# First expert layer of a mixture-of-experts kernel in seven block products, with seeded PSUM banks and streamed block sums

## The chip, the cores and the metric

The kernel runs on one core of a Trainium2 chip. The metric is the device time of one execution in microseconds (us); I quote medians. TensorE is called PE below, VectorE DVE, ScalarE ACT, GpSimd POOL, the sequencer that issues transfers SP, as in the profile.

## The reference

Linear attention produces x of 4608 x 512, an eight-round normalisation gives each token a weight P for each of 8 experts, and every token goes through every expert:

```python
out = np.zeros((N, D), dtype=np.float32)          # N = 4608, D = 512
for e in range(E):                                # E = 8
    h = np.maximum(x @ w1[e], 0.0)                # w1[e]: 512 x 1024   "first layer"
    ye = h @ w2[e]                                # w2[e]: 1024 x 512   "second layer"
    out += P[:, e:e + 1] * ye
```

The two products per expert are nearly all of the work. The kernel computes in fp16 with fp32 sums.

## The kernel before

The work of the experts is cut into units: one expert, one group of 512 tokens, so 72 units. In experts 1 to 7 the second layer is already done as a two-by-two block product with seven block products in place of eight (Strassen's scheme in Winograd's form): sums of blocks of h and w2 are formed first (`S` and `T`), and one accumulated PSUM bank may serve several output blocks. (PSUM holds the sums that PE makes; a bank is one 128 x 512 fp32 tile of it here. To evict a bank is to read its result out.) The first layer is plain, with x held transposed on chip (`xT`):

```python
def layer1(e, g):
    ...
    for f in range(NFT):                           # 8 feature tiles of 128
        def f_hq(_, ...):
            for c in range(NDT):                   # 4 contraction tiles of 128
                nc.tensor.matmul(ghq["tile"], lhsT=gw1["tile"][:, c, ts(f, P)],
                                 rhs=xT[c][:, ds(512 * g, 512)], start=(c == 0), stop=(c == NDT - 1))
        def f_rl(_, ...):
            nc.scalar.activation(out=gh["tile"][:, f, :], in_=ghq["tile"], func=AF.Relu)
        t1 = add(("pe", 0.87), f_hq, deps=[...], acq=[ghq], use=[gw1], prio=...)
        ...
```

The second layer runs twice per unit, once for each half of the tokens (`sub(0)`, `sub(1)`), each half in two banks of its own. VectorE evicts with one instruction that scales by P and adds into the accumulator in SBUF:

```python
def sub(s):
    gX, gY = S_.grp(p_ye[2 * s]), S_.grp(p_ye[2 * s + 1])
    ...
    m1 = pm(A(1, 1), Bq(1, 1), X, True, th[0:4], True, 0.0);   e1 = ev(X, 0, 0, m1)
    m5 = pm(SS(1), T(1), Y, True, [tS[0]], True, 0.1);         e5 = ev(Y, 1, 1, m5)
    m2 = pm(A(1, 2), Bq(2, 1), Z, False, ...);                 ev(Z, 0, 0, m2)
    m6 = pm(SS(2), T(2), X, False, [tS[1], e1], ...);          e6 = ev(X, 0, 1, m6)
    ...                                            # m3, m7, m4: 7 products, 7 evictions per half
```

Nobody writes the order of instructions down. Each `add` records a task with an engine, an assumed duration and its dependencies, and a planner in the kernel plays the tasks through and emits them in the order in which they would start. The semaphores are put in afterwards, from what each emitted instruction reads and writes; for PSUM they go by whole banks.

The softmax here doesn't subtract the row's maximum and nothing guards it: scores larger than these inputs give would overflow.

Of the kernel before, what the change touches and what calls it, by code (L numbers as in the profile page):

```python
# [8 lines left out]

# [107 lines left out]
def kernel(  # L117
# [36 lines left out]
    sk = ctx.enter_context(tc.tile_pool(name="sk", bufs=1))  # L154

    xT = [const.tile([P, N], FP16, tag=f"xT{c}", name=f"xT{c}") for c in range(NDT)]
# [18 lines left out]
    p_T, p_S = S_.pool(2), S_.pool(2)  # L175
# [48 lines left out]
    def att(b, g):  # L224
# [140 lines left out]
        for c2 in range(2):  # L365
            gx = S_.grp(p_att)

            def f_xt(_, c2=c2, gx=gx):
                gx["tile"] = aps.tile([P, S], FP16, tag="att", name="xt_ps")
                for i in range(5):  # L370
                    nc.tensor.transpose(gx["tile"][:, 64 * js[i]:64 * js[i] + P],  # L371
                                        gxn["tile"][:, i, 2 * c2:2 * c2 + 2, :].rearrange("p r e -> p (r e)"), ident)

            def f_xc(e, c2=c2, gx=gx):
                copy(e, xT[2 * g + c2][:, S * b:S * b + S], gx["tile"])
            t1 = fadd(("pe", 0.3), f_xt, deps=txn, acq=[gx], use=[gxn], prio=pr)
            xt_done[(b, 2 * g + c2)] = fadd({"act": 0.64, "dve": 0.46}, f_xc, deps=[t1], use=[gx], prio=pr)

    lg_done = []

    def logits(b2):
        gl = S_.grp(p_att)

        def f_l(_):
            gl["tile"] = aps.tile([P, NJ, E], FP32, tag="att", name="lg_ps")
            for i in range(NJ):
                for c in range(NDT):
                    nc.tensor.matmul(gl["tile"][:, i, :], lhsT=xT[c][:, ts(NJ * b2 + i, P)], rhs=wg_sb[:, c, :],  # L388
                                     start=(c == 0), stop=(c == NDT - 1))

        def f_x(_):
            nc.scalar.activation(out=P0_sb[:, NJ * b2:NJ * b2 + NJ, :], in_=gl["tile"], func=AF.Exp)
        t1 = add(("pe", 1.0), f_l, deps=[xt_done[(b, c)] for b in (2 * b2, 2 * b2 + 1) for c in range(NDT)],
                 acq=[gl], prio=-50.0)
        lg_done.append(add(("act", 0.3), f_x, deps=[t1], use=[gl], prio=-50.0))
# [85 lines left out]
    accp = []  # L481

    def f_close(_):
        front.close()
        accp.append(ctx.enter_context(tc.tile_pool(name="accp", bufs=1)))
        for g in range(NA, NG):
            acc[g] = accp[0].tile([P, 4, 512], FP32, tag=f"acc{g}", name=f"acc{g}")
        accp.append(ctx.enter_context(tc.tile_pool(name="combo", bufs=2)))
    t_close = add(("none", 0.0), f_close, deps=front_ids, prio=0.0)
# [6 lines left out]
    def layer1(e, g):  # L496
        gw1, tw1, gw2, tw2 = w_t[e]
        ui = e * NG + g
        bs = range(512 * g // S, (512 * g + 511) // S + 1)
        xd = [xt_done[(b, c)] for b in bs for c in range(NDT)] if e == 0 else []  # L500
        th = []
        gh = S_.grp(p_h)

        def f_ha(_):
            gh["tile"] = hpool.tile([P, NFT, 512], FP16, tag="h", name="h")
        tha = add(("none", 0.0), f_ha, deps=[prev_hq[0]], acq=[gh], prio=ui - 400.0)
        for f in range(NFT):
            use_att = e > 0 and f % 2 == 1
            ghq = S_.grp(p_att if use_att else p_hq)

            def f_hq(_, f=f, ghq=ghq, use_att=use_att):
                ghq["tile"] = (aps if use_att else hqp).tile([P, 512], FP32, tag="att" if use_att else "hq", name="hq")
                for c in range(NDT):
                    nc.tensor.matmul(ghq["tile"], lhsT=gw1["tile"][:, c, ts(f, P)], rhs=xT[c][:, ds(512 * g, 512)],  # L514
                                     start=(c == 0), stop=(c == NDT - 1))

            def f_rl(_, f=f, ghq=ghq):
                nc.scalar.activation(out=gh["tile"][:, f, :], in_=ghq["tile"], func=AF.Relu)  # L518
            t1 = add(("pe", 0.87), f_hq, deps=[tw1[f // 4], prev_hq[0]] + xd, acq=[ghq], use=[gw1], prio=ui + 0.1 * f + 0.35)
            prev_hq[0] = t1  # L520
            th.append(add(("act", 0.6), f_rl, deps=[t1, tha], use=[ghq, gh], prio=ui - 400.0))
        return gh, th
# [10 lines left out]
    def unit_plain(e, g):  # L533
        gw1, tw1, gw2, tw2 = w_t[e]
        gh, th = layer1(e, g)
        gy = [S_.grp(p_ye[tt % 2]) for tt in range(4)]
        ty = [None] * 4
        for tt in range(4):
            for half in range(2):
                def f_y(_, half=half, tt=tt):  # L540
                    if half == 0:
                        gy[tt]["tile"] = yps.tile([P, 512], FP32, tag=f"ye{tt % 2}", name=f"ye{tt % 2}")
                    for f in range(4 * half, 4 * half + 4):
                        nc.tensor.matmul(gy[tt]["tile"], lhsT=gh["tile"][:, f, ds(P * tt, P)], rhs=gw2["tile"][:, f, :],  # L544
                                         start=(f == 0), stop=(f == NFT - 1))
                ty[tt] = add(("pe", 0.87), f_y, deps=[tw2[half], ty[tt]] + th[4 * half:4 * half + 4],
                             acq=[gy[tt]] if half == 0 else [], use=[gw2, gh],
                             prio=e * NG + g + 0.1 * (2 * tt + half) + 0.65)
# [25 lines left out]
    def combos(e):  # L574
        gw1, tw1, gw2, tw2 = w_t[e]
        gT = S_.grp(p_T)
        last = None
        for i in range(4):
            def f_T(_, i=i):
                if i == 0:  # L580
                    gT["tile"] = accp[1].tile([P, 4, 4, 256], FP16, tag="T", name="T")
# [6 lines left out]
            last = add(("dve", 0.6), f_T, deps=tw2 + [t_close, last], acq=[gT] if i == 0 else [], use=[gw2, gT],  # L588
                       prio=NG * e - 4.0)
        return gT, last  # L590

    def unit(e, g, gT, tT):
        gw1, tw1, gw2, tw2 = w_t[e]
        ui = e * NG + g
        gh, th = layer1(e, g)
        gS = S_.grp(p_S)
        tS = []
        for i in range(4):
            def f_S(_, i=i):
                if i == 0:  # L600
                    gS["tile"] = accp[1].tile([P, 4, 4, 2, P], FP16, tag="S", name="S")
# [7 lines left out]
            tS.append(add(("dve", 0.62), f_S, deps=th + tS[-1:] + [t_close], acq=[gS] if i == 0 else [],  # L609
                          use=[gh, gS], prio=ui - 399.0))  # L610
        def sub(s):
            gX, gY = S_.grp(p_ye[2 * s]), S_.grp(p_ye[2 * s + 1])
# [13 lines left out]
            def pm(lhs, rhs, region, first, deps, acq, prio):  # L626
                g_, col = region

                def f_m(_):
                    if acq:  # L630
                        n = 2 * s + (0 if g_ is gX else 1)
                        g_["tile"] = yps.tile([P, 2, 256], FP32, tag=f"ye{n}", name=f"ye{n}")
                    for kk in range(4):
                        nc.tensor.matmul(g_["tile"][:, col, :], lhsT=lhs(kk), rhs=rhs(kk),  # L634
                                         start=(first and kk == 0), stop=(kk == 3), skip_group_check=True)
                return add(("pe", 0.44), f_m, deps=tw2 + [tT] + deps, acq=[g_] if acq else [],
                           use=[gw2, gT, gh, gS, g_], prio=ui + 0.3 + prio + 0.02 * s)

            def ev(region, ti, dh, dep):
                g_, col = region  # L640
                gg = 4 * g + 2 * s + ti

                def f_e(_):
                    dst = acc[g][:, 2 * s + ti, 256 * dh:256 * dh + 256]
                    nc.vector.scalar_tensor_tensor(out=dst, in0=g_["tile"][:, col, :], scalar=P_sb[:, gg, e:e + 1],  # L645
                                                   in1=dst, op0=ALU.mult, op1=ALU.add)
# [3 lines left out]
            X, Z, Y = (gX, 0), (gX, 1), (gY, 0)  # L650
            m1 = pm(A(1, 1), Bq(1, 1), X, True, th[0:4], True, 0.0)
            e1 = ev(X, 0, 0, m1)
            m5 = pm(SS(1), T(1), Y, True, [tS[0]], True, 0.1)
            e5 = ev(Y, 1, 1, m5)
            m2 = pm(A(1, 2), Bq(2, 1), Z, False, th[4:8] + [m1], False, 0.05)
            ev(Z, 0, 0, m2)
            m6 = pm(SS(2), T(2), X, False, [tS[1], e1], False, 0.2)
            e6 = ev(X, 0, 1, m6)
            m3 = pm(SS(4), Bq(2, 2), Y, False, [tS[3], e5], False, 0.3)
            ev(Y, 0, 1, m3)  # L660
            m7 = pm(SS(3), T(3), X, False, [tS[2], e6], False, 0.4)
            e7 = ev(X, 1, 1, m7)
            m4 = pm(A(2, 2), T(4), X, False, th[4:8] + [e7], False, 0.6)
            ev(X, 1, 0, m4)
# [6 lines left out]
    w_t[1] = load_w1(1, prio=0.0, after=60.0) + load_w2(1, prio=0.0, after=70.0)  # L671
    for e in range(E):
        if e >= 2:
            w_t[e] = load_w1(e, prio=float(e), deps=w_t[e - 1][1][1:]) + load_w2(e, prio=float(e), deps=w_t[e - 1][3][1:])
        if e > 0:
            gT, tT = combos(e)
        for g in range(NG):
            if e == 0 or (e == E - 1 and g == NG - 1):
                unit_plain(e, g)
            else:  # L680
                unit(e, g, gT, tT)
# [31 lines left out]
```

## Time and profile before

| | before |
|---|---|
| time, median (lowest to highest) | 1029.81 us (1029.41 to 1031.32, 4 runs) |
| PE busy, share of the profiled span | 98% |
| DVE, ACT, POOL busy | 69%, 42%, 4% |
| a steady unit | 13.02 us |

A busy PE in this profile includes a tail of about 0.17 us after each group of matmuls (1.04 us are shown for eight that are followed by the next after 0.87). The pace must be read from starts, and the time from one start to the next that leaves no gap is called a slot below. Between the products whose bank is evicted and reused, the kernel before has first-layer matmuls to put. This is its timeline right after the product called N6 below (columns: start, duration, engine, line, operation, operands, count):

```profile
506.31 1.03 PE L514 MATMUL hq<-xT,w 128*128 128x512 f16 x4
507.17 1.04 PE L634 MATMUL ye<-w,S 128*128 128x256 f16 x8
508.04 1.04 PE L634 MATMUL ye<-T,S 128*128 128x256 f16 x8
```

N6 ended its slot at 506.31; N7, the third line, starts 1.73 us later. The first two lines are independent work that fills the eviction's time.

### The profile page before, as it was taken

How to read it: one execution, taken by the hardware profiler on the slowest of the kernel's cores; microseconds unless marked ns; L12 is line 12 of the kernel's file. 1: busy time of each engine (PE TensorE's matmuls, PEld its weight loads, DVE VectorE, ACT ScalarE, POOL GpSimd, SP SyncE). 2: the span in 40 equal slices, each digit the busy share in tenths (PEclk: the TensorE clock that was granted, in tenths of full speed). 3: DMA queues.
4: the chain of work that ended last, by engine and by line, in shares of the span. 5: the costliest groups of instructions: out<-in, count | busy, mean ns of one | idle time of the engine just before them, and what ended most of it. 6: DMA issues, size and time to landing. Idle time of an engine off the chain costs nothing.

```text
span 1033.2 us, 17328 instructions
## 1 busy us (share of the span) xinstructions
PE 1014.5 (98%) x7202; PEld 646.7 (63%) x7202; DVE 713.9 (69%) x1501; ACT 432.4 (42%) x714; POOL 41.6 (4%) x47
## 2 busy tenths in 40 slices
PE   7898999999999999999999999999999999999998
PEld 3554664466666666666666666666666666666664
DVE  6897958566666766676666766676666766666664
ACT  4886844543333333333333333333333333333332
POOL 4221100000000000000000000000000000000000
PEclk9898999999999999999999999999999999999999
DMA  9997400140005000040005000050004100013333
GB/s 263 341 257 255 150 2 1 17 66 2 1 1 83 1 1 2 4 79 1 1 1 79 3 1 1 1 83 1 1 1 64 19 1 1 1 31 81 80 81 98
DMA packets 31743, 55.65 MB, mean 54 GB/s; under 512 B 2736, under 2 KB 11952, under 8 KB 31664
## 3 DMA queue, kind: packets, MB, share of 16 engines
q0 software_dynamic: 14480, 20.33, 11.4%
q1 hardware_dynamic: 16864, 33.69, 10.7%
q8 instruction: 56, 0.92, 0.4%
q10 hardware_dynamic: 320, 0.52, 0.1%
q14 instruction: 23, 0.19, 0.1%
HBM read 61.88 MB, written 9.44 MB: 69 GB/s over the span
## 4 chain that ended last, share of the span: by engine, by line
PE 92%; DVE 4%; DMA 2%; ACT 1%; issue 0%; DVEq 0%; ACTq 0%
PE hq L514 47%; PE ye L634 37%; PE ye L544 5%; DMA kin<-in_k_dram 2%; PE qt_ps L316 1%; PE num_ps L355 1%; PE xt_ps L371 1%; PE kv_ps L290 1%; DVE xn L360 1%; DVE tq L266 1%; DVE gs L420 0%; PE lg_ps L388 0%; PE den_ps L331 0%; PE cs_ps L425 0%; DVE eq L264 0%
## 5 line engine op out<-in xcount | busy, mean ns | idle before, releaser
L518 ACT ACTIVATE h<-hq 128x512 f16<-128x512 f32 x576 | 343.5, 597 | 548.5 <-PE hq L514 548.3
L514 PE MATMUL hq<-xT,w 128*128 128x512 f16 x2304 | 560.9, 381 | 0.2 <-ACT h L518 0.2
L645 DVE SCALAR_TENSOR_TENSOR acc<-ye,P_sb,acc 128x256 f32<-128x256 f32 x868 | 391.3, 484 | 143.3 <-PE ye L634 143.3
L514 PEld LDWEIGHTS <-w 128*128 128x128 f16 x2304 | 225.0, 98 | 199.8 <-issue 5.4
L634 PEld LDWEIGHTS <-S 128*128 128x128 f16 x1984 | 194.1, 98 | 48.9
L634 PE MATMUL ye<-T,S 128*128 128x256 f16 x1488 | 192.8, 273 | 0.0
L634 PEld LDWEIGHTS <-h 128*128 128x128 f16 x1488 | 145.6, 98 | 57.6
L608 DVE TENSOR_TENSOR S<-h 128x1024 f16<-128x1024 f16 x124 | 85.5, 689 | 112.3 <-ACT h L518 112.3
L634 PE MATMUL ye<-w,h 128*128 128x256 f16 x992 | 129.4, 273 | 0.0
L544 PE MATMUL ye<-w,h 128*128 128x512 f16 x320 | 79.2, 385 | 0.0
L634 PE MATMUL ye<-T,h 128*128 128x256 f16 x496 | 65.1, 273 | 0.0
L634 PE MATMUL ye<-w,S 128*128 128x256 f16 x496 | 64.3, 273 | 0.0
L544 PEld LDWEIGHTS <-h 128*128 128x128 f16 x320 | 30.3, 99 | 32.3 <-issue 1.4
L608 DVE TENSOR_TENSOR S<-h,S 128x1024 f16<-128x1024 f16 x62 | 42.5, 686 | 0.0
L608 DVE TENSOR_TENSOR S<-S,h 128x1024 f16<-128x1024 f16 x62 | 42.3, 682 | 0.0
L194 POOL DMA_DIRECT2D w<-in_moe_w_dram x18 | 14.9, 829 | 665.7 <-PE hq L514 628.5
L360 DVE TENSOR_TENSOR xn<-num_ps,rden 128x512 f16<-128x512 f32 (+1 forms) x48 | 26.7, 596 | 5.3 <-PE num_ps L355 4.8
L212 POOL CAST vv<-vin 128x1152 f16<-128x1152 f32 x16 | 21.2, 1325 | 85.8 <-DMA vin<-in_v_dram 63.0
L561 DVE TENSOR_SCALAR acc<-acc,P_sb 128x512 f32<-128x512 f32 x36 | 15.1, 490 | 12.4 <-ACT acc L208 12.3
L253 ACT ACTIVATE ek<-kin 128x1152 f16<-128x1152 f32 x16 | 18.6, 1161 | 8.7 <-DMA kin<-in_k_dram 8.6
L208 ACT COPY acc<-ye 128x512 f32<-128x512 f32 x27 | 15.8, 586 | 14.7 <-PE ye L544 14.7
L355 PE MATMUL num_ps<-kvz,qpT 128*128 128x128 f16 x160 | 15.9, 230 | 4.8 <-DVE rden L337 3.7
(66 smaller groups left out, 327.1 us busy)
## 6 DMA issues: line engine op xcount, KB each, us to landing
w<-in_moe_w_dram POOLq DMA_DIRECT2D x14, 1024.0 KB, 9.5
out_dram<-acc SPq DMA_DIRECT2D x68, 128.0 KB, 2.3
kin<-in_k_dram SPq DMA_DIRECT2D x14, 576.0 KB, 6.9
qin<-in_q_dram SPq DMA_DIRECT2D x14, 576.0 KB, 5.8
vin<-in_v_dram SPq DMA_DIRECT2D x14, 576.0 KB, 6.8
w<-in_moe_w_dram POOLq DMA_DIRECT2D x4, 512.0 KB, 7.8
kin<-in_k_dram POOLq DMA_DIRECT2D x2, 576.0 KB, 11.5
qin<-in_q_dram POOLq DMA_DIRECT2D x2, 576.0 KB, 12.2
```

Of the source, the lines that this page charges most:

```text
L208: nc.scalar.copy(out=dst, in_=src)
L212: nc.gpsimd.tensor_copy(out=dst, in_=src)
L253: nc.scalar.activation(out=ge["tile"], in_=gin[nm]["tile"], func=AF.Exp)
L355: nc.tensor.matmul(gn["tile"][:, i - i0, :, hh, :], lhsT=gq["tile"][:, hh, js[i]:js[i] + 2, :].rearrange("p j w -> p (j w)"), rhs=gz["tile ...
L360: nc.vector.tensor_tensor(out=gxn["tile"][:, i0:i1], in0=gn["tile"][:, 0:i1 - i0].rearrange("p i r h e -> p i (r h) e"), in1=grd["tile"][: ...
L514: nc.tensor.matmul(ghq["tile"], lhsT=gw1["tile"][:, c, ts(f, P)], rhs=xT[c][:, ds(512 * g, 512)], start=(c == 0), stop=(c == NDT - 1))
L518: nc.scalar.activation(out=gh["tile"][:, f, :], in_=ghq["tile"], func=AF.Relu)
L544: nc.tensor.matmul(gy[tt]["tile"], lhsT=gh["tile"][:, f, ds(P * tt, P)], rhs=gw2["tile"][:, f, :], start=(f == 0), stop=(f == NFT - 1))
L561: nc.vector.tensor_scalar(out=acc[g][:, tt, :], in0=acc[g][:, tt, :], scalar1=P_sb[:, gg, 0:1], scalar2=None, op0=ALU.mult)
L608: nc.vector.tensor_tensor(out=Sx[:, i], in0=a0, in1=a1, op=op)
L634: nc.tensor.matmul(g_["tile"][:, col, :], lhsT=lhs(kk), rhs=rhs(kk), start=(first and kk == 0), stop=(kk == 3), skip_group_check=True)
L645: nc.vector.scalar_tensor_tensor(out=dst, in0=g_["tile"][:, col, :], scalar=P_sb[:, gg, e:e + 1], in1=dst, op0=ALU.mult, op1=ALU.add)
```

## The change

The intent: one eighth of the first layer's matmul work goes in 63 of 72 units. The parts:

- First layer in seven products of blocks of 256 tokens (`block7`), in two pairs of feature tiles. Sums of w1 blocks (`W`) are made on VectorE once per expert, sums of x blocks once in expert 0, written to a DRAM scratch (`xd`) and loaded again for every unit, in place of keeping x on chip.
- A product that serves two output blocks (M1, N1) is no longer read twice: ScalarE copies its bank into a second PSUM bank ("seed"), and the next product accumulates on the copy.
- Both token halves of the second layer now share banks (`ye0`, `ye1`, and one seeded bank), because the first layer needs a seeded bank too and the kernel, as before, has eight banks in use.
- Three of fourteen evictions a unit go over ScalarE (scaled copy to SBUF) and GpSimd (add).

The core of the diff, cut:

```diff
-    xT = [const.tile([P, N], FP16, ...) for c in range(NDT)]
+    xT = xp.tile([P, NDT, N], FP16, tag="xT", name="xT")
+    xd = [dpool.tile([P, NXB], FP16, tag=f"xd{g}", name=f"xd{g}") for g in range(NG)]     # in DRAM
...
+    def x_load(e, g):
+            nc.sync.dma_start(out=gr["tile"], in_=xd[g])                    # 128 x 3584 fp16
...
+    def block7(e, g, gW, tW):
+        def pair(gi):
+            m1 = pm(A(1, 1, gi), B11, gX, True, ...)
+            a1 = acts(f_seed, [m1], [gX], [gZ])            # nc.scalar.copy(out=Zt[1], in_=gX["tile"])
+            m5 = pm(W(1, gi), T(1), gR, True, [m1, tW], 0.05)
+            a5 = acts(f_s5, [m5, ...], [gR], [gs5])        # copy to SBUF
+            m2 = pm(A(1, 2, gi), B21, gZ, False, [a1], 0.1)
+            th[0].append(acts(f_h11, [m2], [gZ, gh]))      # relu
+            m6 = pm(W(2, gi), T(2), gX, False, [a1, tW], 0.08)
+            a2 = acts(f_s2, [m6, ...], [gX], [gs2])        # copy to SBUF
+            m3 = pm(W(4, gi), B22, gR, False, [a5], 0.12)
+            th[1].append(add(("dve", 0.8), f_h12, deps=[m3, a2], ...))      # add and relu
+            m7 = pm(W(3, gi), T(3), gX, False, [a2], 0.14)
+            d22 = add(("dve", 0.8), f_h22, deps=[m7, a5], ...)              # add and relu
+            m4 = pm(A(2, 2, gi), T(4), gX, False, [d22], 0.16)
+            th[0].append(acts(f_h21, [m4], [gX, gh]))      # relu
+        pair(0)
+        pair(1)
...
-            e1 = ev(X, 0, 0, m1)
+            c1 = add(("act", 0.48), f_seed, deps=[m1], acq=[gZ], use=[gX], prio=ui - 400.0)
-            ev(Z, 0, 0, m2)
+            ev(gZ, 0, 0, m2, split=True)                   # over ScalarE and GpSimd
...
-            ev(X, 1, 0, m4)
+            ev(gX, 1, 0, m4, split=(s == 1))
```

## The prediction

> **What bounds the kernel now.** I read the busy table first, then the chain that ended last, then a stretch of the timeline in the middle of the run. The page of the kernel before says:
>
> ```profile
> PE 1014.5 (98%) x7202; PEld 646.7 (63%) x7202; DVE 713.9 (69%) x1501; ACT 432.4 (42%) x714; POOL 41.6 (4%) x47
> ...
> PE hq L514 47%; PE ye L634 37%; PE ye L544 5%; DMA kin<-in_k_dram 2%; PE qt_ps L316 1%; PE num_ps L355 1%; PE xt_ps L371 1%; PE kv_ps L290 1%; DVE xn L360 1%; DVE tq L266 1%; DVE gs L420 0%; PE lg_ps L388 0%; PE den_ps L331 0%; PE cs_ps L425 0%; DVE eq L264 0%
> ...
> L514 PE MATMUL hq<-xT,w 128*128 128x512 f16 x2304 | 560.9, 381 | 0.2 <-ACT h L518 0.2
> L645 DVE SCALAR_TENSOR_TENSOR acc<-ye,P_sb,acc 128x256 f32<-128x256 f32 x868 | 391.3, 484 | 143.3 <-PE ye L634 143.3
> ```
>
> TensorE (PE) carries the chain and hardly waits: 0.2 us in front of 2304 first-layer matmuls (L514). A full PE can still be a stalling one, so the timeline of a steady unit (one expert, 512 tokens) has to show the pace. The columns are start, duration, engine, line, operation, count:
>
> ```profile
> 501.96 1.04 PE L634 MATMUL ye<-w,h 128*128 128x256 f16 x8
> 502.21 0.60 ACT L518 ACTIVATE h<-hq 128x512 f16<-128x512 f32 x1 [0.32 <-PE hq L514]
> 502.60 1.79 DVE L645 SCALAR_TENSOR_TENSOR acc<-ye,P_sb,acc 128x256 f32<-128x256 f32 x4
> ...
> 502.83 1.04 PE L634 MATMUL ye<-T,S 128*128 128x256 f16 x8
> ...
> 503.70 1.89 PE L514 MATMUL hq<-xT,w 128*128 128x512 f16 x8
> ...
> 505.43 1.04 PE L634 MATMUL ye<-T,S 128*128 128x256 f16 x8
> ...
> 514.98 1.04 PE L634 MATMUL ye<-w,h 128*128 128x256 f16 x8
> ```
>
> Eight matmuls of 256 columns are followed by the next group after 502.83 - 501.96 = 0.87 us: 108.8 ns each. Eight of 512 columns take 505.43 - 503.70 = 1.73 us: 216.5 ns each. The pattern comes back after 514.98 - 501.96 = 13.02 us. A unit has 56 second-layer matmuls of 256 (seven products instead of eight are already used there) and 32 first-layer matmuls of 512: 56 x 0.1088 + 32 x 0.2165 = 6.09 + 6.93 = 13.02 us. So there is no gap at all: now the only bound is the number of columns streamed.
>
> The same lines give latencies that I need below. A group's last result is readable about 0.20 us after the group's slot ends (four matmuls from 501.96 fill 0.435 us, VectorE starts at 502.60). Four evictions of 256 columns take 1.79 us, a pitch of 0.447 and 0.484 for the last. From an engine that ends to a PE that waited for it takes 0.05 us, as here (0.60 from 1022.95, then 1023.60):
>
> ```profile
> 1022.95 0.60 ACT L518 ACTIVATE h<-hq 128x512 f16<-128x512 f32 x1 [0.27 <-PE hq L514]
> 1023.60 0.98 PEld L544 LDWEIGHTS <-h 128*128 128x128 f16 x6 [0.53 <-ACT h L518]
> ```
>
> **What the Trainium skill says.** "TensorE: Matmul & The Clock Gate", Back-to-back issue gap, gives N/2.4 + 2.5 ns warm: 109.2 and 215.8 ns; the trace agrees (108.8, 216.5). So two matmuls of 256 cost hardly more than one of 512, and the narrower form is not a loss in itself. "ScalarE: Activation LUTs", What ACT_TABLE_LOAD costs, gives 186 ns + 0.833 ns per column, 93 more with a pointer operand, and a 93 ns overlap back to back. For 512 columns that is 612 ns; the trace has 597 for the relu and 586 for the copy into acc, a little less. For 256 columns, which the trace lacks for ScalarE, I take 0.39 us for a copy and 0.49 with a pointer scale (estimates from that page, the first lowered by what the trace shows). "PSUM — Partial Sum Buffer", PSUM bank collisions, says that no two of TensorE, VectorE and ScalarE may touch one bank in the same quadrant at once, even on different columns, so guards go by bank. No run here tests that, but the built program agrees: its waits join both halves of a bank. This becomes the main point.
>
> **The change part by part.** *Removed from PE:* one of eight products in 63 units. First layer after: 56 x 0.1088 = 6.09 in place of 6.93 us, 0.84 us a unit. If everything stays hidden, 63 x 0.84 = 53 us go, to 977 us.
>
> *VectorE:* evictions go from 14 to 9 a unit (the seed makes M1's second reader unnecessary, and 3 go to ScalarE and GpSimd): -5 x 0.447 = -2.2 us. Added: four add-relu instructions of 512 columns; the nearest thing in the trace, the 512-column eviction, took 751 ns, so about +2.9. Per expert four 1024-column sums of w1 at 0.69, 0.3 us a unit. Together 9 x 0.447 + 4 x 0.6 (the S sums, at their pitch) + 2.9 + 0.6 = 9.9 us a unit: below 12.2, busier, not the bound.
>
> *ScalarE:* 8 relus of 597 ns (4.8 us) become 2 x (seed copy, two copies to SBUF, two relus) x 0.59 = 5.9, plus two 256-column seeds (0.8) and three scaled copies (1.5): 8.2 us. No bound either, but now *between* matmuls that depend on each other.
>
> *Transfers:* per unit 128 x 3584 x 2 B = 0.92 MB of block sums. The hardware queue moved 33.69 MB in 10.7% of 1033 us, 305 GB/s: 3 us plus a landing, asked for nearly a unit ahead. Hidden. The 36 small sums in expert 0 (about 0.4 us of VectorE each, 14 us) lie where PE still does all eight products; up to 3 us may show.
>
> *Moved: the waits.* Here I chose to go by the order of the built program, in which most units have the same PE sequence. Call the first-layer products M (pairs a and b of feature tiles), the second-layer ones N (both token halves). Slots are 0.435 us for an M and 0.87 for an N:
>
> M1b, N7, M5b, N3, N4, M6b, M2b, M3b, M7b, M1a', M5a', M6a', M4b, M2a', M3a', M7a', N1, half N5, N2, half N5, N6, M4a': 14 x 0.435 + 7 x 0.87 = 12.18 us.
>
> Four places in it cannot keep that pace:
>
> 1. N7 overwrites the bank of N6, and waits until both halves are evicted: 0.20 + 0.447 + 0.484 + 0.05 = 1.18 us after N6. Between stand M4 and M1b, 0.87. Stall 0.31.
> 2. M7b waits for the copy of M6b. In ScalarE's order a scaled copy of N4 stands before it, and that waits for VectorE's eviction of N4's other half in the same bank. From the end of N4: 0.20 + 0.484 + 0.05 + 0.40 (pitch of the scaled copy) + 0.586 + 0.05 = 1.77. M6b, M2b, M3b fill 1.305. Stall 0.47.
> 3. M6a' reuses the bank of M1a' and waits for its seed copy: 0.20 + 0.586 + 0.05 = 0.84; only M5a' (0.435) lies between. Stall 0.40.
> 4. N2 waits for two seeds of N1. The first seed waits for both halves of N1 (same bank), the second for the first: 0.20 + 0.39 + 0.05 + 0.39 + 0.05 = 1.08; half N5 fills 0.435. Stall 0.64.
>
> The other dependent places I walked the same way; they come out even or with slack (the add-relu before M4b ends 0.6 us early). Sum 1.82 us: the unit becomes 12.18 + 1.82 = 14.0 us against 13.02. About three units of each expert, where the next expert's sums are made, have another order, in which the first stall is partly filled; I take an average of 13.95. That is 62 x 0.93 = +58 us. The last unit saves 0.84 and stalls about as much: 0. The start of expert 1, where first-layer groups stand nearly alone, and expert 0's extra sums: +3. Total 1030 + 58 + 3 = 1091, said as 1090.
>
> **The rivals.** *The waits are hidden and PE stays at its pace:* 977 us. For it: VectorE (9.9) and ScalarE (8.2) have room, and the schedule was made with an eye to such latencies. Against it: the four stalls above follow from semaphores in the built program, each a sum of durations, not from how busy an engine is. Cutting them in half gives 13.1 us a unit, about 1035 us: a draw. *VectorE becomes the bound:* the add-relu is a custom instruction not in the trace. At twice my 0.72 us it adds 2.9: 12.8 us a unit, by itself about 1017; together with the stalls 1100 or more. GpSimd's adds may block VectorE's two-input sums for some tenths: "SBUF — State Buffer", Who interferes with whom, says the second to issue waits when both read SBUF through the shared port; GpSimd does no adds in the trace before, so it shows nothing on this. *The stream starves PE:* it would need landings of over 12 us; the 1 MB weight loads took 9.5 with conversion on another queue. I give it little; it would put a unit at 14 to 15 us.
>
> **How the range follows.** The stalls rest on measured durations, except for the copy from PSUM to PSUM. If it takes 0.50 and 0.33 instead of 0.59 and 0.39, stalls 3 and 4 shrink by 0.09 and 0.12, and with a shorter second one the unit is 13.75: 1077. If half of the second is filled as well: 1063. Contention on VectorE at each expert's start: up to 1115. So 1062 to 1115. For faster by over 2% the stalls would have to be under about 0.5 us a unit, a quarter of my sum: 9%. For a draw between 0.5 and 1.2: 9%.
>
> **What would show it.** If right: PE busy falls well under 98%, with idle in front of the first-layer group (L617) put down to ScalarE and in front of the second-layer group (L801) put down to ScalarE and VectorE; steady units repeat about every 14 us, with gaps of 0.3 to 0.65 us before N7, M7b, M6a' and N2; slots stay at 0.435 and 0.87; no wait on the streamed x. It is wrong if PE shows no gaps at these four places, if copies from PSUM to PSUM take well under 0.5 us, or if the waits are elsewhere: before M4 (the add-relu) or on the transfer.

## The result, and the profile after

| | before | after |
|---|---|---|
| time, median | 1029.81 us | 1078.12 us (1077.77 to 1079.71, 4 runs) |
| PE busy us, matmuls | 1014.5 (98%), 7202 | 1000.6 (93%), 8716 |
| DVE / ACT / POOL busy | 69 / 42 / 4% | 71 / 55 / 16% |
| a steady unit | 13.02 us | 13.94 us |

The ratio is 1.0469 with a 95% interval of 1.0451 to 1.0488: slower.

The page after, its busy line and its chain that ended last by engine:

```profile
PE 1000.6 (93%) x8716; PEld 791.9 (73%) x8716; DVE 769.1 (71%) x1507; ACT 589.7 (55%) x1150; POOL 177.3 (16%) x233
...
PE 66%; DVE 14%; ACT 13%; issue 5%; DMA 1%; ACTq 0%; DVEq 0%; POOLq 0%
```

No engine is full, and the chain that was 92% PE is now a third DVE, ACT and hand-overs. That is the picture of a chain of waits, not of a new busiest engine. This is the PE side of one steady unit of the kernel after, from the timeline (same columns; a bracket gives the idle time before the row and what ended it):

```profile
502.61 1.04 PE L801 MATMUL ye<-w,h 128*128 128x256 f16 x8
...
503.48 0.60 PE L801 MATMUL ye<-T,S 128*128 128x256 f16 x4
...
504.48 1.03 PE L801 MATMUL Zye<-w,h 128*128 128x256 f16 x8 [0.40 <-ACT Zye L836]
...
506.66 1.04 PE L617 MATMUL hq<-xs,w 128*128 128x256 f16 x8
...
507.79 1.03 PE L801 MATMUL ye<-T,S 128*128 128x256 f16 x8
...
511.72 0.60 PE L617 MATMUL att<-xs,W 128*128 128x256 f16 x4
...
512.62 0.60 PE L617 MATMUL hq<-xs,W 128*128 128x256 f16 x4 [0.31 <-ACT s L633]
...
513.49 0.60 PE L617 MATMUL att<-xs,W 128*128 128x256 f16 x4
...
514.37 0.60 PE L617 MATMUL hq<-xs,W 128*128 128x256 f16 x4 [0.28 <-ACT Zye L629]
...
516.55 1.04 PE L801 MATMUL ye<-w,h 128*128 128x256 f16 x8
```

The names are those of the prediction; a prime marks a product of the next unit. Four matmuls of 256 columns fill a slot of 0.435 us, eight fill 0.87. So the true gaps are: before N2 (third row) 504.48 - 503.48 - 0.435 = 0.57 us; before N7 (fifth row) 507.79 - 506.66 - 0.87 = 0.26; before M7b 512.62 - 511.72 - 0.435 = 0.47; before M6a' 514.37 - 513.49 - 0.435 = 0.45. Together 1.75 us, and 12.18 + 1.75 is, to 0.01, the measured period of 516.55 - 502.61 = 13.94 us. (Starts to the nanosecond give 109.15 ns a matmul, so 12.22 us of slots and 1.72 of gaps.) Note two traps: the bracket understates each gap by the tail of 0.17 us, and the gap before N7 has no bracket at all, since the tail covers most of it.

The chain of waits in order of time, in the same unit (start, duration, engine, tile, line), shows what stands in each gap:

```profile
503.68 0.36 ACT Zye L836
...
504.07 0.36 ACT Zye L836
...
507.26 0.49 DVE acc L816
...
511.05 0.49 DVE acc L816
...
511.62 0.31 ACT st L823
...
512.00 0.58 ACT s L633
...
513.75 0.58 ACT Zye L629
```

Two seed copies one after the other, the second eviction of N6, then an eviction, a scaled copy and a copy in a row (N4 to M7b), then the seed copy of M1a'. These are the four places of the prediction.

### The profile page after: what moved, and what is told of

It is laid out like the page before. It is cut to its first block, busy times and chain, and to the rows that moved or that the text cites. A ratio compares the mean times of both kernels' runs of the same rounds, so it can differ in the third digit from the quotient of the medians. Undisturbed runs are those within 1.5% of the kernel's fastest.

```text
span 1077.9 us, 21504 instructions
## 1 busy us (share of the span) xinstructions
PE 1000.6 (93%) x8716; PEld 791.9 (73%) x8716; DVE 769.1 (71%) x1507; ACT 589.7 (55%) x1150; POOL 177.3 (16%) x233
## 3 DMA queue, kind: packets, MB, share of 16 engines
q1 hardware_dynamic: 32128, 99.76, 28.0%
## 4 chain that ended last, share of the span: by engine, by line
PE 66%; DVE 14%; ACT 13%; issue 5%; DMA 1%; ACTq 0%; DVEq 0%; POOLq 0%
PE ye L801 28%; PE hq L617 14%; DVE acc L816 7%; PE Zye L801 6%; PE att L617 5%; PE ye L693 4%; ACT Zye L836 4%; ACT Zye L629 3%; PE Zye L617 3%; PE hq L526 3%; ACT s L633 3%; ACT st L823 2%; DMA qin<-in_q_dram 1%; DVE xst L558 1%; DVE tk L274 1%
## 5 line engine op out<-in xcount | busy, mean ns | idle before, releaser
L816 DVE SCALAR_TENSOR_TENSOR acc<-ye,P_sb,acc 128x256 f32<-128x256 f32 x558 | 251.0, 480 | 120.8 <-PE ye L801 119.8
L826 POOL TENSOR_TENSOR acc<-acc,st 128x256 f32<-128x256 f32 x186 | 137.2, 751 | 683.0 <-ACT st L823 683.0
L617 PEld LDWEIGHTS <-W 128*128 128x128 f16 x2016 | 196.5, 97 | 70.2 <-issue 47.7
L617 PE MATMUL hq<-xs,W 128*128 128x256 f16 x1008 | 150.9, 272 | 29.3 <-ACT Zye L629 14.6
L617 PEld LDWEIGHTS <-w 128*128 128x128 f16 x1512 | 147.8, 98 | 19.8 <-issue 1.9
L617 PE MATMUL att<-xs,W 128*128 128x256 f16 x1008 | 151.2, 273 | 0.0
L617 PE MATMUL hq<-xs,w 128*128 128x256 f16 x1008 | 143.7, 272 | 0.8 <-DVE h L646 0.8
L646 DVE CUSTOM_DVE_ANT_0 h<-att,s 128x512 f16<-128x512 f32 x126 | 86.4, 686 | 40.0 <-ACT s L633 31.5
L643 ACT ACTIVATE h<-hq 128x512 f16<-128x512 f32 x126 | 75.6, 600 | 54.7 <-PE hq L617 54.7
L646 DVE CUSTOM_DVE_ANT_0 h<-hq,s 128x512 f16<-128x512 f32 x126 | 86.9, 689 | 4.9 <-PE hq L617 4.9
```

What stands on the lines that cost most here:

```text
L617: nc.tensor.matmul(dst[:, p, :], lhsT=lhs(p, c), rhs=rhs(c), start=(first and p == 0 and c == 0), stop=(c == 1), skip_group_check=True)
L643: nc.scalar.activation(out=hd(1, 0), in_=gX["tile"], func=AF.Relu)
L646: nc.vector._custom_dve(TENSOR_ADD_SAT, out=dst, in0=ps, in1=sb, s0=3.0e38, s1=0.0)
L816: nc.vector.scalar_tensor_tensor(out=dst(), in0=bank(g_), scalar=P_sb[:, gg, e:e + 1], in1=dst(), op0=ALU.mult, op1=ALU.add)
L826: nc.gpsimd.tensor_tensor(out=dst(), in0=dst(), in1=gst["tile"], op=ALU.add)
```

## The experiments

All kernels below gave correct results. Those called "same PE order" were compared with the kernel after, instruction by instruction: the sequence of matmuls on PE is identical, so only waits differ.

### swap_half: which half of N4's bank is read first (same PE order)

```diff
-            ev(gX, 1, 0, m4, split=(s == 1))
+            ev(gX, 1, 0, m4, split=(s == 0))
```

> One token changed: of the two halves of N4's bank, ScalarE reads the first and VectorE the second, in place of the other way round. The order on PE stays the same. Theory (dependent waits by bank): ScalarE's scaled copy no longer waits for VectorE's eviction, so from the end of N4 to M7b it takes 0.20 + 0.38 + 0.58 + 0.05 = 1.21 us against 1.305 us of matmuls between: the gap of 0.46 us before M7b goes in the some 45 units with the usual order, the other three gaps stay; unit 13.94 -> 13.48, total about 1057 us. Rival (the matmuls themselves, the load on ScalarE, VectorE and GpSimd, or the stream set the pace): the work is the same on every engine, so 1078 us within 3.

Measured: 1057.43 us, ratio to before 1.0262 (1.0233 to 1.0291). The steady unit is 13.47 to 13.48 us. Its timeline:

```profile
504.56 0.47 ACT L823 ACTIVATE st<-ye,P_sb 128x256 f32<-128x256 f32 x1 [1.22 <-PE ye L801]
...
504.94 0.59 ACT L633 COPY s<-hq 128x512 f32<-128x512 f32 x1
...
505.61 0.60 PE L617 MATMUL hq<-xs,W 128*128 128x256 f16 x4
```

The scaled copy now waits for PE, no longer for DVE, and M7b (third row) starts without a gap. The 44 steady intervals lose 0.465 us each, 20.5 us; the medians differ by 20.7. Nothing was taken from any engine: the cost was the position of one wait.

### one_seed: one seed copy of 512 columns for two of 256 (same PE order)

```diff
             def f_seed(_):
-                nc.scalar.copy(out=bank(gZ), in_=bank(gX))
+                if s == 0:
+                    nc.scalar.copy(out=Zt[0], in_=gX["tile"])
```

> The two chained 256-column seed copies of the second layer are one copy of 512 columns; the order on PE stays. Theory: before N2 the wait is 0.20 + 0.58 + 0.05 - 0.435 = 0.40 us in place of the 0.57 us in the trace; 62 x 0.17 = 10.5 us less, about 1067 us; the other three gaps stay. Rival (ScalarE's busy time counts): it loses only 62 x (0.71 - 0.58) = 8 us of busy time out of 590, and is idle 45%, so nothing, 1078.

Measured: 1074.05 us, ratio to before 1.0419 (1.0395 to 1.0444): only 4 us less than after in place of 10.5.

```profile
502.79 0.60 PE L801 MATMUL ye<-T,S 128*128 128x256 f16 x4
503.61 1.03 PE L801 MATMUL Zye<-w,h 128*128 128x256 f16 x8 [0.22 <-ACT Zye L837]
504.48 1.47 PE L801 MATMUL ye<-T,S 128*128 128x256 f16 x12
505.79 1.04 PE L617 MATMUL hq<-xs,w 128*128 128x256 f16 x8
506.99 1.03 PE L801 MATMUL ye<-T,S 128*128 128x256 f16 x8 [0.16 <-DVE acc L816]
```

The gap before N2 is 503.61 - 502.79 - 0.435 = 0.39 us, as expected (0.40). But the gap before N7 grew from 0.26 to 506.99 - 505.79 - 0.87 = 0.33. DVE starts N6's eviction 0.28 us after the end of its slot here, 0.20 in the kernel after. There are two candidates. The built program makes that eviction wait for two engines, PE and ACT, where after waits for PE alone; and GpSimd's first add is just ending at that moment. The traces tell them apart. The chain shows the wait for PE as an instruction of its own (`DVEq`) in front of the eviction:

```profile
506.00 0.02 DVEq L816
...
506.07 0.13 DVE acc L816
```

In all 57 evictions of this kind, 0.093 to 0.094 us pass from PE's signal to the start, against 0.024 to 0.026 for those that wait for PE alone. In 11 of the 57 no GpSimd add is ending near the start, and the delay is the same; joint's trace below has five evictions with the same two waits and GpSimd idle, and they take 0.093 to 0.095. So it is the second wait, and its 0.07 us is the whole growth. The steady unit is 13.84 us, 0.10 shorter than after, and the 61 intervals from the first N1 to the last lose 5.9. Of the two us more that the medians lose, 1.3 lie before the first N1 (215.26 us against 213.96), in front of every changed instruction.

### double_stream: the transfers doubled (same PE order)

```diff
             nc.sync.dma_start(out=gr["tile"], in_=xd[g])
+            nc.sync.dma_start(out=xdup, in_=xd[g])
```

> After each load of block sums the same 0.92 MB are copied once more, to another DRAM buffer: DMA traffic of the stream doubled in read and added in write. Theory: the loads (4.6 us to landing, asked for about 12 us ahead) stay hidden, 1078 us within 4. Rival (the stream from DRAM costs the time): at least 20 us more.

Measured: 1079.55 us, ratio 1.0472 (1.0445 to 1.0499), against 1.0469 for after. The page has the queue (packets, MB, share of 16 engines) and the loads (count, size, us to landing):

```profile
q1 hardware_dynamic: 34144, 157.57, 40.5%
...
xs<-xd SPq DMA_DIRECT2D x63, 896.0 KB, 4.6
```

58 MB more than the 99.76 MB of after, and the loads still land in 4.6 us. The stream is free here.

### double_seed: the first layer's seed copy made twice (same PE order)

```diff
             def f_seed(_):
                 nc.scalar.copy(out=Zt[1], in_=gX["tile"])
+                nc.scalar.copy(out=Zt[1], in_=gX["tile"])
```

> The first layer's seed copy is made twice (the second writes the same again); the order on PE is that of the after kernel. Theory: M6a' waits for the second copy, which comes 0.49 to 0.62 us later (pitch of a 512-column copy, or its whole duration and a wait for the first), so the gap of 0.44 us there grows to 0.93 to 1.06; M6b has 3 us between and hides it. In the some 46 units of the usual order that is 23 to 29 us, up to 38 if every unit pays: total 1101 to 1116. Rival (that gap is filled elsewhere, or ScalarE's time is simply idle): below 1085.

Measured: 1116.60 us, ratio 1.0838 (1.0813 to 1.0862). This one ran on another chip than the other experiments; the kernel before took 1030.69 us there.

```profile
512.33 0.60 PE L617 MATMUL att<-xs,W 128*128 128x256 f16 x4
513.81 0.60 PE L617 MATMUL hq<-xs,W 128*128 128x256 f16 x4 [0.88 <-ACT Zye L630]
```

The gap before M6a' is 513.81 - 512.33 - 0.435 = 1.05 us, 0.60 more than the 0.45 of after, and the steady unit grew from 13.94 to 14.54. The second copy waits for the first (start to start it took 0.60 us), so the upper end of the expectation held, and nearly all units pay. The time of this copy goes one for one into the unit, although ACT is busy only half of the time. The other pair's seed copy was doubled as well and adds no gap to a steady unit: other matmuls fill that time.

### joint_two: the same instructions, planned with the waits that the chip has

In the kernel after, the planner treats the two token halves of a bank as independent tasks: N2's first half may start after the first seed copy, and N7's first half after the first eviction. The emitted program cannot do that, since its semaphores go by bank. Here both halves of each product are one task, each reader depends on it, and the next writer depends on both readers:

```diff
-            def pm(lhs, rhs, g_, new, deps, prio):            # per half: 4 matmuls, 0.44
+        def pm(lhs, rhs, g_, new, deps, prio):                # both halves: 8 matmuls, 0.88
...
-                t = add(("pe", 0.44), f_m, deps=..., prio=ui + 0.3 + prio + 0.02 * s)
+            return add(("pe", 0.88), f_m, deps=tw2 + [tT] + deps, ..., prio=ui + 0.3 + prio)
...
-            m7 = pm(SS(3), T(3), gX, False, [tS[2], e6], 0.4)   # e6: this half's eviction
+        m7 = pm(SS(3), T(3), gX, False, [tS[2]] + e6, 0.4)      # e6: both evictions
...
+        # f_seed: both copies as one task of 0.96; the scaled copy of a bank depends on the
+        # VectorE eviction of its other half; GpSimd's add is assumed at 0.8 in place of 0.96
```

> Same instructions in the same numbers; only the order differs: in the planning the two token halves of each second-layer product are one task, and the readers of a bank's two halves wait for both, as the chip's semaphores have it. Theory: the gaps in the after kernel come from an order that was made as if the halves of a bank were independent; with the true waits known, other matmuls are put into most of the gaps: units of 12.2 to 12.6 us, total 985 to 1010 us, faster than before (1030). Rival (two matmuls of 256 need more than one of 512, or the added work of ScalarE, VectorE, GpSimd and DMA is what costs): over 1060 us.

Measured: 992.51 us, ratio to before 0.9630 (0.9607 to 0.9652). The busy line of its page, and the timeline around N2:

```profile
PE 966.4 (98%) x8716; PEld 791.9 (80%) x8716; DVE 774.0 (78%) x1507; ACT 586.7 (59%) x1150; POOL 181.7 (18%) x233
...
511.99 1.04 PE L796 MATMUL ye<-T,S 128*128 128x256 f16 x8
512.86 0.60 PE L617 MATMUL hq<-xs,w 128*128 128x256 f16 x4
513.30 1.04 PE L796 MATMUL Zye<-w,h 128*128 128x256 f16 x8
```

PE has the same 8716 matmuls, DVE, ACT and POOL the same 1507, 1150 and 233 instructions as after, and it is 86 us faster. A whole N5 and a first-layer product now stand in front of N2 (third row): 511.99 to 513.30 is 1.31 us, exactly three slots of 0.435, so the seed copies cost nothing there. From the first N1 at 212.86 us to the last at 967.31, 61 intervals average 12.37 us, against the pure slots' 12.22.

Counted from the starts in the traces, from 225 us on, PE's gaps sum to 95 us in after (51 before M6a', 46 before M7b, 56 before N2, 56 before N7, and some small ones) and to 9 us in joint_two. The difference is the measured 86 us.

The planner itself can be asked what it expected, by running it with the instruction calls stubbed out (a computation, not a run). Its plan of the kernel after ends at 1004 us, where the chip took 1078. It has one gap in a steady unit, 0.40 us before M6a', 51 times as on the chip, and none before M7b, N2 or N7. Its plan of joint_two ends at 999 us, where the chip took 992.5. So three of the four waits are ones that the planner did not know. The fourth it knew and accepted; joint_two has it 12 times.

### second_only: the second-layer part on the old first layer

```diff
     # in short: layer1 as in the kernel before (8 products, xT on chip); unit(): the second layer of after
-            m1 = pm(A(1, 1), Bq(1, 1), gX, True, th[s], 0.0)
+            m1 = pm(A(1, 1), Bq(1, 1), gX, True, th[0:4], 0.0)
```

> The second-layer part of the change alone (seed copies, three evictions a unit over ScalarE and GpSimd, both token halves in one bank) on the old first layer with eight products and x kept on chip. No product is saved. Theory: the old first-layer products are independent of each other and are put between N1 and N2 (two of 0.87 us and more), so the seed gap is filled; between N6 and N7 stands one of 0.87 us against the 1.18 us that the evictions of both halves need, so a gap of 0.26 to 0.31 us a unit stays: 13.02 -> 13.3 us, 62 x 0.29 = 18 us, total about 1048. Rival (the gain of VectorE's lighter load shows by itself): 1030 or less. Rival (the seeds and split evictions are what costs, whatever stands between): +62 x (0.57 + 0.26) = 51 us, about 1080.

Measured: 1046.28 us, ratio 1.0159 (1.0130 to 1.0188), within 2% of before, but clear of noise.

```profile
501.95 1.91 PE L645 MATMUL ye<-T,S 128*128 128x256 f16 x16
503.69 1.03 PE L519 MATMUL hq<-xT,w 128*128 128x512 f16 x4
504.82 1.03 PE L645 MATMUL ye<-T,S 128*128 128x256 f16 x8
```

One first-layer product of 0.87 us stands between N6 (the second half of the first row) and N7 (the third): the gap is 504.82 - 503.69 - 0.87 = 0.26 us, and no other steady one is left. 62 x 0.26 = 16 us is the whole difference. So putting both halves into one bank costs a little by itself; the seed copies cost nothing while independent matmuls are at hand (from 510.90 us sixteen of the first layer stand between N1 and N2, which starts at 514.36 without a gap). The new first layer has fewer of these, because its own seven products depend on each other, and in after the planner did not put them there.

### joint, joint_vec4, joint_light: looking for the best version

All three keep joint_two's planning with one seed copy of 512 columns in place of two. joint changes nothing else; joint_vec4 gives N4's second half back to VectorE; joint_light also gives N2's first half back.

```diff
         # joint
-            for s in range(2):
-                nc.scalar.copy(out=Zt[0][:, s, :], in_=gX["tile"][:, s, :])
+            nc.scalar.copy(out=Zt[0], in_=gX["tile"])
         # joint_vec4
-        ev(gX, 1, 0, m4, split=(1,))
+        ev(gX, 1, 0, m4, split=())
         # joint_light, besides
-        ev(gZ, 0, 0, m2, split=(0, 1))
+        ev(gZ, 0, 0, m2, split=(1,))
```

> As joint_two (halves planned as one task, 992.5 us), and the two seed copies of 256 columns are one of 512. Theory: the seed gap is filled already, so 0.18 us shorter on its chain gives nothing or little: 988 to 995 us. Rival (the seed chain still stands in the critical path): 62 x 0.18 = 11 us less, about 981.

Measured: 996.48 us, ratio 0.9667 (0.9645 to 0.9688), 1.5 us past the expectation: 4 us more than joint_two. The shorter chain gave nothing. The shorter task makes the planner choose other orders, and before L617 there is more waiting for the seed copy of the first layer (6.9 us in all against 4.1, tails left out): the gap before M6a' stands 23 times in this trace and 12 times in joint_two's, 4.5 us more. The stubbed planner says the same: 23 times against 12, and a plan 5 us longer.

> As joint, and N4's second half is evicted by VectorE alone, not by ScalarE and GpSimd: 62 x 0.45 = 28 us more busy time on VectorE (774 -> 802 us of some 990), 62 x 0.47 = 29 less on ScalarE. Theory: neither engine is the bound, fewer waits across engines on one bank: 985 to 992 us. Rival (VectorE's load is the next bound): above 995.

Measured: 995.16 us, ratio 0.9655 (0.9634 to 0.9677): no gain over joint beyond noise. That is past the expected 985 to 992 and, by its number, just inside the rival's "above 995". DVE is 79% busy in it, 782 us where 802 were expected. joint_light, with more work on DVE, decides against the rival.

> As joint_vec4, and N2's first half also goes back to VectorE, so that one eviction of 14 a unit goes over ScalarE and GpSimd: VectorE about 830 us busy. Theory: 983 to 992 us, near the floor of 977. Rival (VectorE's load is the next bound): above 995.

Measured: 989.81 us, ratio 0.9611 (0.9582 to 0.9639), in the expected range.

```profile
PE 965.2 (98%) x8716; PEld 791.7 (80%) x8716; DVE 812.2 (82%) x1631; ACT 524.9 (53%) x964; POOL 87.6 (9%) x109
```

With DVE at 82% it is the fastest of all, so DVE's load is not the next bound. It beats the kernel before by 3.9% and the kernel after by 8.2% (0.9611 / 1.0469 = 0.918, across two sets of rounds). From joint_two it differs by 0.2 to 0.3% with overlapping intervals; I would call the two equal.

## Why the prediction was right

The predicted time was 1090 us in a range of 1062 to 1115, with 9% each left for faster and for a draw; measured were 1078.12, slower. Point by point:

- **PE's pace in narrow matmuls.** Predicted 0.1088 us each: slots of 0.435 and 0.87 us appear everywhere in the trace after. The prediction read 108.8 and 216.5 ns from starts of two digits; to the nanosecond its trace gives 109.2 and 215.8. So two of 256 columns cost 2.5 ns more than one of 512, a unit after has 12.22 us of slots, and 0.80 us a unit are really saved, not 0.84.
- **The four waits.** Predicted 0.31, 0.47, 0.40 and 0.64 us, sum 1.82. Measured 0.26, 0.47, 0.45 and 0.57, sum 1.75. The first was too long because 1.79 us / 4 is not the pitch of evictions that wait for nothing: in the trace before, a pair takes 0.88 us, a pitch of 0.40. The third was too short because that copy starts 0.25 us after the slot, not 0.20, with a wait of its own in front as in one_seed. In the fourth, the second copy starts 0.39 us after the first and takes 0.357, where the prediction had 0.39 for each and 0.05 between. These errors nearly cancel, which is luck; the places and the causes are not. The experiments confirm them apart: in a steady unit swap_half removes the second and only that, one_seed shortens the fourth as computed, double_seed lengthens the third one for one, second_only leaves the first alone standing.
- **What does not count.** Transfers: double_stream. Busy time of ACT, DVE and POOL: joint_two has all of it and is 8% faster than after. The add-relu took 0.69 us, predicted 0.72. The longest wait that I feared from GpSimd did not appear in the S sums: 0.687 us each after, 0.689 before. But only 5 of 248 S sums overlap a GpSimd add there. In joint 63 do, and then the wait is real (first line joint, second joint_light, with a third of the adds):

```profile
L769 DVE TENSOR_TENSOR S<-h 128x1024 f16<-128x1024 f16 x124 | 92.5, 746 | 77.7 <-ACT h L643 77.5
L769 DVE TENSOR_TENSOR S<-h 128x1024 f16<-128x1024 f16 x124 | 85.3, 688 | 29.2 <-ACT h L643 27.2
```

In the 31 cases where the add began first, the sum took 0.83 to 1.22 us; in the 32 where the sum began first it kept its 0.68 to 0.69. That agrees with the page cited in the prediction: the second to issue waits. PE waited for S sums less than 1 us in all, so it costs little even there.
- **The sum.** Units were to add 62 x 0.93 = 58 us, the start 3, the end 0. In the traces, the 61 intervals from the first N1 to the last take 839.8 us (213.96 to 1053.78) after and 795.1 (211.19 to 1006.27) before: +44.7, 13 less than predicted. In these two traces the start adds 2.8, and the end gives 2.8 back. But the profiled execution of before took 1035.18 us, 5.4 above its median, and all its intervals but the first are steady, so the excess lies elsewhere. By the medians, start and end together add 48.3 - 44.7 = 3.6; how they share it is not shown.

The mis-sized term is the average of 13.95 us a unit. The steady units are right (13.94, predicted 14.0). What I passed over with "about three units of each expert ... have another order, in which the first stall is partly filled" are 15 intervals at five changes of expert, which take 12.33, 13.88 and 13.47 us in turn, 13.23 on average: (13.95 - 13.23) x 15 = 11 us, most of these 13 (and so of the miss of 12 in the total). They hold 104, 120 and 112 matmuls, so their slots are 11.3, 13.1 and 12.2 us and their gaps 1.0, 0.8 and 1.3 where a steady unit has 1.75. In these units, another order already hides a part of the waits, which was the hint that the order was the matter at all.

The prediction's step from semaphores to stalls held. What it did not ask is why a planner that knows durations would leave such gaps. joint_two answers it: the planner's dependencies were by half a bank, the program's waits are by bank. Three of the four gaps come from that. The fourth, before M6a', was in the plan, and stays where nothing else is put there.

## What to carry to other kernels

When one instruction stream is planned ahead, the plan must contain the waits that will be emitted, not those that the data need: with semaphores by PSUM bank, tasks that share a bank are one task. Saving work on the bound engine can make it wait instead, above all when the work saved was independent and what replaces it is a chain; walk each reuse of a bank as a sum of durations, and ask what stands between. An engine that is busy half of the time can still be on the path with some of its instructions, as ACT's first seed copy of a unit is here.

## What the Trainium skill lacked or had wrong

- "Perfetto Trace Analysis", Identifying the Most-Contended Engine, takes MFU and the LDWEIGHTS (weight load) busy share as the good measures of how near a kernel is to its bound, and matmul busy time as a bad one. Here the weight-load share rose from 63% to 73% while the kernel became 4.7% slower, since the same product in 256 columns needs twice the loads; matmul busy, 98% to 93%, pointed the right way. Between these two kernels, of different matmul shapes, the share misleads.
- "TensorE: Matmul & The Clock Gate", Back-to-back issue gap, gives about 131 ns as a sustained figure for 512 columns. In this case's streams it is 215.8 ns, which is that page's other formula.
- On the pages that I read I found no hand-over times between engines. Here a group's result is taken up about 0.20 us after its slot ends, PE resumes about 0.05 us after the engine that it waited for, and an eviction that waits for two engines can start 0.094 us after the signal in place of 0.025 (57 cases in one_seed).
- "PSUM — Partial Sum Buffer", PSUM bank collisions, says that a bank must be guarded as a whole, reads against reads included, but not what it costs: one scaled copy that had to wait for another engine's read of the other half of the bank cost 0.465 us a unit, 21 us of 1078.
- "ScalarE: Activation LUTs", Step-by-step: what each stage is for, calls PSUM the faster target without a figure. A copy of 512 columns took 579 ns into PSUM and 583 to 588 into SBUF.
